# Two halves of three rounds for four pairs of rounds: regrouping the small-tile transforms of a spectral filter beside an MLP

## The chip, the cores and the metric

The kernel runs on one core of a Trainium2 chip. The metric is the device time of one execution in microseconds, as the median of several runs. The core has a matrix engine (TensorE, PE in the profile, with its weight loads shown apart as PEld), VectorE (DVE), ScalarE (ACT), GpSimd (POOL) and a queue engine (SyncE, SP) that issues the DMAs here, those that transpose among them. TensorE writes to PSUM, eight banks of 512 float32 per partition; the other engines copy from there.

## The reference

```python
def _A_ref(x, w_r, w_i):
    X = rfft2(x.astype(float32), axes=(-2, -1))
    X = X * (w_r + 1j * w_i)
    return irfft2(X, s=(S, D), axes=(-2, -1)).astype(bfloat16)

def _B_ref(x, w1, b1, w2, b2):
    h = gelu(einsum("bsd,df->bsf", x, w1) + b1)      # tanh form
    return einsum("bsf,fd->bsd", h, w2) + b2

xn = layernorm(x)                                    # x: 1 x 2048 x 640, bfloat16
return x + _A_ref(xn, w_r, w_i) + _B_ref(xn, w1, b1, w2, b2)   # F = 1536
```

The output is the sum of the input, a spectral filter of its normalized form and a two-layer MLP of the same normalized form.

## The kernel before

The 2048 rows lie in 16 tiles of 128 rows. Every operation has a name with its tile, pair of tiles or group, and a table (`ORDER`) says by hand in which order each of the five engines issues its operations; a second table (`SLOTS`) says which PSUM bank or piece of on-chip memory each buffer gets. `Plan.sync` works out the waits: an operation waits for the writers of what it reads and for the last users of the memory that it writes. Nothing is scheduled beyond that: if an operation waits, all behind it on its engine wait too.

Normalization and transposes. `st`, `ag`, `ve`, `rs`, `nm` normalize a tile (VectorE, with a little on GpSimd). Tiles 0 to 5 are transposed by TensorE (`tp`) and copied (`tc`), tiles 6 to 15 by DMA on the SP queue (`td`), into `xnT`.

The MLP. `h` is layer 1, in blocks of tiles (`BLOCKS`): a matmul takes 128 rows of W1 by 128 features as weights and streams 128 columns for each tile of the block; `ge` is the gelu on ScalarE. `k` and `l` are layer 2. For the tiles of `KEEP` it runs early and is stored (`k`, added to the input by `kk` on VectorE); for the others (`l`) it stays in PSUM until the filter's last matmul (`fin`) adds to it. A group of `k` or `l` is three matmuls of 512 columns and three of 128.

The filter. The two-dimensional transform is made of matmuls with tables:

- `f1`, `f2` fold the rows (VectorE), `G` is a transform over the 128 rows of a tile, `gx` copies its result to `XV`.
- `b0` to `b5` transform along the width, for two or three tiles at a time (`GROUPS`); each fills the four low PSUM banks, and two copies `xb` (one for two banks) empty them into `Xb`.
- `c` finishes the transform across tiles, by matmuls of 32 x 32 weights. The array of TensorE holds sixteen such tiles at once, so a pass is 16 matmuls that run side by side. Before, four tiles of the 16 (`P` = 0 to 3) form a round pair: `cP.0` and `cP.1`, each of two passes of 322 columns that add up in the four low banks. Each round is emptied by two copies `y`.
- `m` multiplies with the complex filter, `z` sums the products (VectorE).
- `d` goes back across tiles, in two rounds of two passes of 320 columns for each `P`; `u` empties them, and `vt` turns the tiles by DMA on the SP queue into `XV`.
- `e0` to `e5` transform the width back, for the tiles of `GROUPS`, again into the four low banks; they need all sixteen turned tiles. `yo` empties a group, `y2` and `yf` unfold it (VectorE), `fin` is the last transform, and `os` adds all up on VectorE before the store `out`.

Since `b`, `c`, `d` and `e` all use the four low banks, one of them can begin only when the copies of the one before it in the order have ended. Between them the order puts layer 1 (in the high banks) and layer 2 as work that fills the time. At the start, 42 matmuls on zeros (`idle0`) run until the first tile is normalized; the first number of `WARM` counts them.

## Time and profile before

| | |
|---|---|
| median of 3 runs | 149.25 us (148.64 to 151.17) |
| profiled execution | 149.7 us, of which the span is 148.4 |
| TensorE busy | 144.8 us, 1847 matmuls |
| VectorE busy | 110.9 us, 242 instructions |
| ScalarE busy | 82.9 us, 161 instructions |
| layer 1, 256 columns | 300 matmuls |
| small-tile transforms | 512 matmuls in 16 rounds |

The span is the time from the first to the last instruction that the profiler recorded; the execution's own time is 1.3 us longer. Busy times of TensorE overlap, as matmuls are pipelined: for what a stretch costs one takes the distance from its first start to the next stretch's. In a timeline row the first number is the start, the second the length from the first start to the last end, then the engine, the line, the operation with its result and its operands, the tile of the array, the shape and the count. A bracket at the end says how long the engine was idle before the row, and for whom. Weight loads are rows of PEld and overlap the matmuls. A row of SPq is the queue's work of issuing; a DMA lands later.

### The profile page before, as it was taken

The numbers are of one execution on the slowest core, as the hardware profiler recorded it, in microseconds if no ns is written. First come the engines' busy times: TensorE is split into PE (matmuls) and PEld (weight loads), VectorE is DVE, ScalarE is ACT, GpSimd is POOL, SyncE is SP. The second block draws the span as 40 slices with busy tenths as digits, with TensorE's granted clock in tenths as the row PEclk, the third lists the DMA queues.
The fourth block names the chain that finished last, engine by engine and source line by source line (L and its number), as shares of the span: only waits on it lengthen the run. The fifth ranks groups of instructions, "written<-read, shape, count | busy, mean of one in ns | idle before, by whom it ended". The sixth has DMA issues, their size and how long they took to land.

```text
span 148.4 us, 4311 instructions
## 1 busy us (share of the span) xinstructions
PE 144.8 (98%) x1847; PEld 99.4 (67%) x1847; DVE 110.9 (75%) x242; ACT 82.9 (56%) x161; POOL 7.0 (5%) x18
## 2 busy tenths in 40 slices
PE   7999999999999999999999999999999999999994
PEld 7989888888868766666554534345676665655564
DVE  2888999999997799498659759700098898968743
ACT  3649889998984775994555467891624204000000
POOL 2003030222200000000000000000000000000000
DMA  4899999366997993004200460645001122101333
GB/s 133 293 326 406 306 269 178 60 93 164 299 203 128 213 210 134 4 4 88 44 4 7 88 133 4 133 92 115 19 4 44 44 88 95 44 0 49 133 111 110
DMA packets 27882, 18.07 MB, mean 122 GB/s; under 512 B 18904, under 2 KB 26584, under 8 KB 27736
## 3 DMA queue, kind: packets, MB, share of 16 engines
q1 hardware_dynamic: 27840, 17.81, 48.8%
q8 instruction: 14, 0.23, 0.6%
q14 instruction: 4, 0.03, 0.1%
q10 hardware_dynamic: 24, 0.00, 0.0%
HBM read 10.92 MB, written 2.62 MB: 91 GB/s over the span
## 4 chain that ended last, share of the span: by engine, by line
PE 70%; DVE 13%; DMA 6%; SPq 5%; issue 2%; ACT 2%; POOL 1%
PE ps L403 70%; DMA X<-in_A_x_dram 6%; SPq L398 5%; DVE stats L508 4%; DVE T L564 3%; DVE T L560 2%; ACT Xb L413 2%; DVE Z L537 1%; DVE mv L510 1%; POOL rstd L519 1%; DVE T L537 1%; DVE ve L518 0%; DVE U L537 0%; DVE W L772 0%
## 5 line engine op out<-in xcount | busy, mean ns | idle before, releaser
L403 PE MATMUL ps<-xnT,W 128*128 128x256 bf16 (+2 forms) x480 | 58.7, 274 | 0.3 <-DMA W<-in_B_w_dram 0.3
L403 PE MATMUL ps<-W,gT 128*128 128x128 bf16 (+4 forms) x408 | 57.9, 291 | 0.0
L403 PEld LDWEIGHTS ps<-xnT,W 128*128 128x128 bf16 x480 | 40.2, 98 | 12.4 <-issue 1.9
L619 ACT ACTIVATE gT<-ps,b1col 128x256 bf16<-128x256 f32 (+2 forms) x96 | 39.3, 483 | 10.8 <-PE ps L403 10.6
L403 PEld LDWEIGHTS ps<-W,gT 128*128 128x128 bf16 x408 | 30.4, 98 | 22.3 <-issue 1.7
L508 DVE BATCH_NORM_STATS2 stats<-X 128x6 f32<-128x320 bf16 x32 | 14.4, 476 | 2.6 <-DMA X<-in_A_x_dram 2.6
L733 DVE TENSOR_TENSOR Wf<-Wf 128x960 bf16<-128x960 bf16 (+1 forms) x12 | 6.8, 597 | 11.8 <-ACT Wf L413 11.7
L413 ACT ACTIVATE Wf<-ps 128x960 bf16<-128x960 f32 (+1 forms) x8 | 6.9, 902 | 12.8 <-PE ps L403 12.8
L413 ACT ACTIVATE Xb<-ps 128x960 bf16<-128x960 f32 (+1 forms) x9 | 9.8, 1138 | 7.0 <-PE ps L403 7.0
L676 DVE TENSOR_TENSOR T<-Y,Wf 128x1288 bf16<-128x1288 bf16 x16 | 12.4, 824 | 0.5 <-ACT Y L413 0.4
L413 ACT ACTIVATE Y<-ps 128x644 bf16<-128x644 f32 x12 | 8.1, 715 | 3.9 <-PE ps L403 3.9
L761 DVE TENSOR_TENSOR xnT<-ps,X 128x640 f32<-128x640 f32 x8 | 6.6, 820 | 4.7 <-PE ps L403 4.7
L772 DVE TENSOR_TENSOR W<-ps,X 128x640 bf16<-128x640 f32 (+2 forms) x10 | 6.9, 687 | 3.8 <-PE ps L403 3.8
L564 DVE TENSOR_TENSOR T<-T 128x512 bf16<-128x512 bf16 (+1 forms) x32 | 9.1, 312 | 0.2
L413 ACT ACTIVATE XV<-ps 128x1280 bf16<-128x1280 f32 x7 | 8.7, 1243 | 0.1
L772 DVE TENSOR_TENSOR W<-ps,xnT 128x640 bf16<-128x640 f32 x8 | 6.5, 820 | 1.8 <-PE ps L403 1.7
L403 PE MATMUL ps<-getab,XV 32*128 32x160 bf16 (+1 forms) x128 | 7.5, 242 | 0.0
L519 POOL TENSOR_TENSOR rstd<-ve,mhalf 128x2 f32<-128x2 f32 (+1 forms) x8 | 6.1, 763 | 31.1 <-DVE ve L518 31.1
L738 DVE TENSOR_TENSOR Wf<-Wf 128x960 bf16<-128x960 bf16 (+1 forms) x12 | 6.7, 596 | 0.8 <-PE ps L403 0.7
L403 PEld LDWEIGHTS ps<-getab,XV 32*128 32x128 bf16 (+1 forms) x128 | 6.4, 146 | 1.2
L403 PE MATMUL ps<-etab,XV 32*128 32x160 bf16 (+1 forms) x128 | 7.2, 232 | 0.0
L680 DVE TENSOR_TENSOR Z<-T 128x644 bf16<-128x644 bf16 x16 | 7.0, 488 | 0.1
(52 smaller groups left out, 111.6 us busy)
## 6 DMA issues: line engine op xcount, KB each, us to landing
out_dram<-W SPq DMA_DIRECT2D x15, 160.0 KB, 1.8
X<-in_A_x_dram SPq DMA_DIRECT2D x7, 320.0 KB, 8.2
W<-in_B_w_dram SPq DMA_DIRECT2D x10, 192.0 KB, 5.6
W<-in_B_w_dram SPq DMA_DIRECT2D x2, 960.0 KB, 8.7
Wf<-in_A_w_i_dram SPq DMA_DIRECT2D x7, 160.5 KB, 3.9
Wf<-in_A_w_r_dram SPq DMA_DIRECT2D x7, 160.5 KB, 4.5
gtab<-c_G SPq DMA_DIRECT2D x1, 512.0 KB, 7.8
htab<-c_H SPq DMA_DIRECT2D x1, 512.0 KB, 5.0
```

The lines of the kernel that those rows point to most:

```text
L398: return K.op(name, q, lambda e, _: e.dma_start(dst, src), reads=reads, writes=[buf], after=after, dma=sem or name, gate=gate)
L403: ins = e.matmul(o_, lhsT=lw, rhs=rh, start=st, stop=sp_, skip_group_check=True)
L413: return e.activation(dst(), src(), ACT.Copy)
L508: K.op(f"st{c}.{h}", "dve", lambda e, _, c=c, h=h: e.bn_stats(stats[:, c, 6 * h:6 * h + 6], view(X, c * D + H2 * h, [[1, H2]])), reads=[B_ ...
L519: K.op(f"rs{c0}", "pool", lambda e, _, a=a, b=b: e.tensor_tensor(out=rstd[:, a:b], in0=ve[:, a:b], in1=mhalf[:, a:b], op=ALU.pow), reads=[ ...
L564: ring_ops.append(K.op(f"f2{pair}.{k}{i}", "dve", lambda e, _, op=op, x1v=x1v, xfv=xfv, o_=o_, o0=o0, o1=o1, w=w: e.tensor_tensor(out=xfv( ...
L619: K.op(f"ge{bi}.{fc}", "act", lambda e, _, c0=c0, nt=nt, fc=fc, f0=f0, hps=hps: e.activation(gT[:, fc, 128 * c0:128 * (c0 + nt)], psb(hps. ...
L676: filt_ops.append(K.op(f"m{pair}.{k}", "dve", lambda e, _, k=k, Y=Y, TB=TB, pair=pair: e.tensor_tensor(out=view(TT, TB.slot * 8 * KP + k * ...
L680: K.op(f"z{pair}.{r}", "dve", lambda e, _, TB=TB, Z=Z, r=r, op=op: e.tensor_tensor(out=view(Zb, Z.slot * 4 * KP + r * KP, [[2 * KP, 2], [1 ...
L733: K.op(f"y2{gi}.{k}", "dve", lambda e, _, k=k, op=op, yo=yo, y2=y2, n=n: e.tensor_tensor(out=view(Wf, Y2 + y2.slot * 3 * D + (H2 - 1) * k, ...
L738: K.op(f"yf{gi}.{k}", "dve", lambda e, _, k=k, op=op, y2=y2, yf=yf, n=n: e.tensor_tensor(out=view(Wf, YF + yf.slot * 3 * D + (D - 1) * k, ...
L772: K.op(f"os{c}.{o0}", "dve", lambda e, _, c=c, os_=os_, fps=fps, o0=o0, w=w, kept=kept, base=base, home=home if kept else None: e.tensor_t ...
```

## The change

The small-tile transforms are regrouped. Instead of four `P` with two rounds each, there are two halves of two `P` each, and a half has three rounds in `c` and three in `d`. A bank of 512 columns, of which a round had filled 322, now gets up to 484: the first round of a half holds the first part of `P0` and the first 162 columns of its second part, the next holds the remaining 160 and the first part of `P1`, the third holds the second part of `P1` alone. So c0.0, c0.1, c1.0, c1.1 and likewise for `d` have 64 matmuls in four passes, c0.2, c1.2, d0.2, d1.2 have 32 in two. In `d` the pieces are 320 + 160, 160 + 320 and 320 columns.

The products lose a temporary: `m1` goes to the buffer T, `m0` is made in place in Y, and `z` sums in place in Y. A pool of six buffers takes the place of those for Y and Z; there are four places for `xb` instead of two, four for `u` instead of three and four for normalized pairs instead of five. The zero matrix of `idle0`, the identity and the row of biases share a tile with the table of `b` (EB), and the statistics and b2 share one with a `u` buffer (U3). GpSimd zeroes the padding of `xb` in eight small pieces instead of two.

Tiles 8 to 11 are one block of layer 1, so 60 matmuls of 512 columns stand for 120 of 256. The groups of `b` and `e` are (0,3), (3,3), (6,2), (8,3), (11,3), (14,2), so that the first has three tiles and the third two. `idle0` has 38 matmuls. Some copies move between ScalarE and VectorE: both copies of b1 are VectorE's, both of b4 ScalarE's, those of b2 are shared. The order of all engines is new.

```diff
-BLOCKS = [(0, 1), (1, 1), (2, 2), (4, 2), (6, 2), (8, 2), (10, 2), (12, 4)]
+BLOCKS = [(0, 1), (1, 1), (2, 2), (4, 2), (6, 2), (8, 4), (12, 4)]
-GROUPS = [(0, 2), (2, 3), (5, 3), (8, 3), (11, 3), (14, 2)]
+GROUPS = [(0, 3), (3, 3), (6, 2), (8, 3), (11, 3), (14, 2)]
-BYPE = ()
-WARM = (42, 4)
+WARM = (38, 4)
...
+pe:l0.0.0 pe:e0 pe:l0.0.3 dve:yo0.0 act:yo0.1 dve:y20.0 pe:e1 dve:y20.1 pe:l0.0.6 dve:yf0.0 act:yo1.1 dve:yf0.1 pe:l0.0.9 act:yo1.0 pe:fin0.0 pe:e2
+dve:os0.0 dve:y21.1 sp:out0.0 pe:l6.0.0 act:yo2.1 dve:y21.0 act:yo2.0 pe:l6.0.3 dve:yf1.0 dve:yf1.1 pe:l6.0.6 dve:y22.1 pe:fin3.0 dve:y22.0 dve:os3.0
...
+        EB = sb("EB", [128, 4 * KP])
+        etab, warm, ident, b1t = EB, EB[:, 800:928], EB[:, 928:1056], EB[0:NFC, 1056:1184]
...
-        TT = sb("T", [128, 11 * D])
-        Zb = sb("Z", [128, 2 * 4 * KP])
-        U2 = sb("U2", [128, 2 * D])
+        TT = sb("T", [128, 32 * KP + 2 * D])
+        U2 = sb("U2", [128, 4 * KP])
         PS = es.enter_context(nc.psum_tensor("ps", [128, 8 * 512], F32))
 
+        XB = [(xb3, 0, 3), (xb3, 6 * KP, 3), (U2, 0, 2), (EB, 0, 2)]
...
-            ("xn", 5), ("x1", 1), ("xf", 2), ("xb", 2), ("y", 2), ("t", 2), ("z", 2), ("u", 3))]
+        p_xn, p_x1, p_xf, p_xb, p_yz, p_t, p_u = [Pool(k, n) for k, n in (
+            ("xn", 4), ("x1", 1), ("xf", 2), ("xb", 4), ("yz", 6), ("t", 2), ("u", 4))]
...
+        def yz(Y):
+            return 8 * KP + 2 * D + 4 * KP * (Y.slot + 4 if Y.slot < 2 else Y.slot - 2)
...
+        def products(pair):
+            Y, TB = Ys[pair], TBs[pair]
+            m1 = K.op(f"m{pair}.1", "dve", lambda e, _: e.tensor_tensor(
+                out=view(TT, TB.slot * 4 * KP, [[2 * KP, 2], [KP, 2], [1, KP]]), in0=yv(Y, True), in1=wv(pair, 1), op=ALU.mult),
+                reads=[Y, B_w, B_wpad], writes=[TB], after=ring_ops)
+            m0 = K.op(f"m{pair}.0", "dve", lambda e, _: e.tensor_tensor(out=yv(Y, False), in0=yv(Y, False), in1=wv(pair, 0), op=ALU.mult),
+                reads=[Y, B_w, B_wpad], writes=[Y], after=[m1])
+            filt_ops.extend([m1, m0])
+            for r, op in enumerate((ALU.subtract, ALU.add)):
+                def sums(e, _, r=r, op=op):
+                    rows = view(TT, yz(Y) + r * KP, [[2 * KP, 2], [1, KP]])
+                    return e.tensor_tensor(out=rows, in0=rows, in1=view(TT, TB.slot * 4 * KP + r * KP, [[2 * KP, 2], [1, KP]]), op=op)
+                K.op(f"z{pair}.{r}", "dve", sums, reads=[TB, Y], writes=[Y], after=[m0])
...
+        CUT, c_ops = 162, []
+        for half in range(2):
+            P0, P1 = 2 * half, 2 * half + 1
+            for n, pieces in enumerate(([(P0, 0, 0, KP), (P0, 1, 0, CUT)], [(P0, 1, CUT, KP - CUT), (P1, 0, 0, KP)], [(P1, 1, 0, KP)])):
+                cps = K.buf(f"cps{half}_{n}", psum, 4, LOW)
+                at, bank = [0, pieces[0][3]], [[], []]
+                c_ops.append(pe(f"c{half}.{n}", lambda pieces=pieces, cps=cps, at=at: [
+                    (psb(cps.slot + 2 * pp + hi, [[1, w]], at[k], 64 * qq + 32 * (lo ^ pp), 32),
                      part(mtab, 64 * hi + 32 * lo, 32, (P == pp == qq == hi == lo == 0) * 128 + v * 64 + r * 32, [[1, 32]]),
+                     part(xb_at[4 * P + 2 * pp + qq][0], 64 * hi + 32 * lo, 32, xb_at[4 * P + 2 * pp + qq][1] + v * KP + c0, [[1, w]]), v == 0 and k == 0, v == 1)
+                    for v in range(2) for k, (P, r, c0, w) in enumerate(pieces) for pp, qq, hi, lo in tiles],
+                    reads=list({id(B_xb[c]): B_xb[c] for P in sorted({p[0] for p in pieces}) for c in range(4 * P, 4 * P + 4)}.values()) + [B_xbpad, B_m] + ([B_xbpad3] if half else []), writes=[cps]))
+                for P in sorted({p[0] for p in pieces}):
+                    mine = [(at[k], r, c0, w) for k, (q, r, c0, w) in enumerate(pieces) if q == P]
+                    o_, r, c0, w = mine[0][0], mine[0][1], mine[0][2], sum(p[3] for p in mine)
+                    for pp in range(2):
+                        Y = Ys[2 * P + pp]
+                        bank[pp].append(K.op(f"y{2 * P + pp}.{len(Y.writers)}", "act dve",
+                             copy(lambda Y=Y, r=r, c0=c0, w=w: view(TT, yz(Y) + r * KP + c0, [[2 * KP, 2], [1, w]]),
+                                  lambda cps=cps, pp=pp, o_=o_, w=w: psb(cps.slot + 2 * pp, [[512, 2], [1, w]], o_)), reads=[cps], writes=[Y], after=(ring_ops if P else []) + bank[pp]))
+            for pair in range(4 * half, 4 * half + 4):
+                products(pair)
+            for n, pieces in enumerate(([(P0, 0, 0, 2), (P0, 1, 0, 1)], [(P0, 1, 1, 1), (P1, 0, 0, 2)], [(P1, 1, 0, 2)])):
+                dps = K.buf(f"dps{half}_{n}", psum, 4, LOW)
+                at, bank = [0, Q4 * pieces[0][3]], [[], []]
+                pe(f"d{half}.{n}", lambda pieces=pieces, dps=dps, at=at: [
+                    (psb(dps.slot + 2 * pp + qq, [[1, Q4 * w]], at[k], 64 * hi + 32 * lo, 32),
                      part(ntab, 64 * qq + 32 * (lo ^ pp), 32, (P == pp == qq == hi == lo == 0) * 96 + 32 * ((0, 2), (1, 0))[v][r], [[1, 32]]),
+                     part(TT, 64 * qq + 32 * (lo ^ pp), 32, yz(Ys[2 * P + pp]) + (2 * hi + r) * KP + v + i0, [[1, w], [2, Q4]]), r == 0 and k == 0, r == 1)
+                    for r in range(2) for k, (P, v, i0, w) in enumerate(pieces) for pp, qq, hi, lo in tiles],
+                    reads=[Ys[2 * P + pp] for P in sorted({p[0] for p in pieces}) for pp in range(2)] + [B_n], writes=[dps])
+                for P in sorted({p[0] for p in pieces}):
+                    mine = [(at[k], 2 * v + i0, w) for k, (q, v, i0, w) in enumerate(pieces) if q == P]
+                    o0, g, w0 = mine[0][0], mine[0][1], sum(p[2] for p in mine)
+                    for pp in range(2):
+                        U = Us[2 * P + pp]
+
+                        def evac(e, name, U=U, dps=dps, pp=pp, o0=o0, g=g, w0=w0):
+                            for o_, w in ((0, 128), (512, 32)):
+                                ins = copy(lambda: uv(U, o_ + w * g, [[D, 2], [w, w0], [1, w]]), lambda: psb(dps.slot + 2 * pp, [[512, 2], [Q4, w0], [1, w]], o0 + o_ // 4))(e, name)
+                            return ins
+                        bank[pp].append(K.op(f"u{2 * P + pp}.{len(U.writers)}", "act dve", evac, reads=[dps], writes=[U, B_us[2 * P + pp]],
+                                             after=a_ops + ring_ops + xs_ops + c_ops[:3] + bank[pp]))
+            for pair in range(4 * half, 4 * half + 4):
+                turn(pair)
```

On TensorE, at the end of the rounds of `d`, before (Z and ntab are the operands of `d`; xnT and W belong to layer 1, W and gT to layer 2):

```order
213 L403 MATMUL ps<-Xb,mtab 32x322 x32
214 L403 MATMUL ps<-xnT,W 128x512 x5
215 L403 MATMUL ps<-Z,ntab 32x320 x32
216 L403 MATMUL ps<-xnT,W 128x512 x5
217 L403 MATMUL ps<-Z,ntab 32x320 x32
218 L403 MATMUL ps<-xnT,W 128x512 x20
219 L403 MATMUL ps<-Z,ntab 32x320 x32
220 L403 MATMUL ps<-xnT,W 128x512 x5
221 L403 MATMUL ps<-Z,ntab 32x320 x32
222 L403 MATMUL ps<-xnT,W 128x512 x20
```

and after, where T holds the products:

```order
237 L397 MATMUL ps<-T,ntab 32x320 x16
238 L397 MATMUL ps<-T,ntab 32x160 x16
239 L397 MATMUL ps<-T,ntab 32x320 x16
240 L397 MATMUL ps<-T,ntab 32x160 x16
241 L397 MATMUL ps<-xnT,W 128x512 x15
242 L397 MATMUL ps<-T,ntab 32x160 x16
243 L397 MATMUL ps<-T,ntab 32x320 x16
244 L397 MATMUL ps<-T,ntab 32x160 x16
245 L397 MATMUL ps<-T,ntab 32x320 x16
246 L397 MATMUL ps<-xnT,W 128x512 x16
247 L397 MATMUL ps<-T,ntab 32x320 x32
248 L397 MATMUL ps<-xnT,W 128x512 x19
```

A round with 320 columns in two passes has become one with passes of 320 and 160 in turn, and the layer-1 work between the rounds has changed: after the last of 64 (rows 242 to 245, d1.1) come 16 matmuls, the last small round (d1.2) and 19 more, where before d3.1 was followed by 20 and then by layer 2.

On TensorE at the first two groups of the way back (getab and XV belong to `e`), before, from e0 on; three more pairs of layer 2 follow until e1 in row 261:

```order
248 L403 MATMUL ps<-getab,XV 128x160 x16
249 L403 MATMUL ps<-W,gT 128x512
250 L403 MATMUL ps<-W,gT 128x128
251 L403 MATMUL ps<-W,gT 128x512
252 L403 MATMUL ps<-W,gT 128x128
253 L403 MATMUL ps<-W,gT 128x512
254 L403 MATMUL ps<-W,gT 128x128
```

and after, from e0 to e1:

```order
279 L397 MATMUL ps<-getab,XV 128x160 x24
280 L397 MATMUL ps<-W,gT 128x512
281 L397 MATMUL ps<-W,gT 128x128
282 L397 MATMUL ps<-W,gT 128x512
283 L397 MATMUL ps<-W,gT 128x128
284 L397 MATMUL ps<-W,gT 128x512
285 L397 MATMUL ps<-W,gT 128x128
286 L397 MATMUL ps<-getab,XV 128x160 x24
```

e0 has three tiles (24 matmuls) where it had two (16), and three pairs of layer 2 stand between e0 and e1 where there were six.

On the SP queue, before, from tile 10's transpose to the last of them (W is W2 here, Wf the filter, etab the table of `b`):

```order
18 L541 DMA_TRANSPOSE xnT<-T 128x5x128
19 L398 DMA W<-in_B_w_dram 128x6x640
20 L398 DMA Wf<-in_A_w_i_dram 16x5136
21 L398 DMA Wf<-in_A_w_r_dram 16x5136
22 L398 DMA etab<-c_E 128x800
23 L398 DMA Wf<-in_A_w_r_dram 16x5136
24 L541 DMA_TRANSPOSE xnT<-T 128x5x128
25 L541 DMA_TRANSPOSE xnT<-Z 128x5x128 x2
26 L541 DMA_TRANSPOSE xnT<-U 128x5x128 x2
```

and after, from tile 6 on, with the first six loads behind:

```order
16 L540 DMA_TRANSPOSE xnT<-T 128x5x128 x6
17 L392 DMA Wf<-in_A_w_r_dram 16x5136
18 L392 DMA Wf<-in_A_w_i_dram 16x5136
19 L392 DMA EB<-c_E 128x800
20 L392 DMA Wf<-in_A_w_i_dram 16x15x321
21 L392 DMA W<-in_B_w_dram 128x6x640
22 L392 DMA Wf<-in_A_w_i_dram 16x16x321 x2
```

The transposes of tiles 10 and 11 now follow that of tile 9 directly, and those of tiles 12 to 15 stand seven rows further on (row 29), behind all loads of the filter.

267 lines of the change are left out of this document (110 added, 157 removed).

## The prediction

> **What bounds the kernel now.** I read the first and second parts of the profile's page (busy time by engine, the span in slices), then the chain of waits that ended last, then the TensorE timeline, stretch by stretch.
>
> ```profile
> PE 144.8 (98%) x1847; PEld 99.4 (67%) x1847; DVE 110.9 (75%) x242; ACT 82.9 (56%) x161; POOL 7.0 (5%) x18
> PE   7999999999999999999999999999999999999994
> PE 70%; DVE 13%; DMA 6%; SPq 5%; issue 2%; ACT 2%; POOL 1%
> ```
>
> ```profile
> 59.64 25.33 PE ps L403 x433
> 84.99 61.47 PE ps L403 x648
> ```
>
> TensorE is busy in every slice from the second on, and the chain's two longest pieces are TensorE alone, from 59.64 us to 146.46 of a span of 148.4. So a change of this kernel is worth what it takes out of TensorE's stream, plus the waits that it opens or closes there; vector and scalar work counts only where a matmul waits for it.
>
> **Paces.** What a row of the stream costs is the distance to the start of the next row; durations overlap.
>
> ```profile
> 22.10 5.08 PE L403 MATMUL ps<-xnT,W 128*128 128x256 bf16 x45
> 27.08 0.45 PE L403 MATMUL ps<-gtab,T 128*128 128x128 bf16 x5
> ...
> 60.90 1.26 PE L403 MATMUL ps<-xnT,W 128*128 128x256 bf16 x10
> 62.08 0.49 PE L403 MATMUL ps<-Xb,mtab 32*32 32x322 bf16 x32
> 62.51 1.27 PE L403 MATMUL ps<-xnT,W 128*128 128x256 bf16 x10
> 63.70 0.51 PE L403 MATMUL ps<-Z,ntab 32*32 32x320 bf16 x32
> 64.15 1.26 PE L403 MATMUL ps<-xnT,W 128*128 128x256 bf16 x10
> ...
> 87.41 1.25 PE L403 MATMUL ps<-xnT,W 128*128 128x512 bf16 x5
> 88.59 0.51 PE L403 MATMUL ps<-Z,ntab 32*32 32x320 bf16 x32
> ...
> 90.67 4.49 PE L403 MATMUL ps<-xnT,W 128*128 128x512 bf16 x20
> 95.08 0.51 PE L403 MATMUL ps<-Z,ntab 32*32 32x320 bf16 x32
> ```
>
> Layer 1, 256 columns: 45 take 4.98 us and 10 take 1.18, so 35 take 3.80, 0.1086 each; the ten lose 1.18 - 1.086 = 0.094 going into a round. 512 columns: 20 take 4.41, 5 take 1.18, so 0.2153 each, and again some 0.10 at the entry. A round of 32 small matmuls costs 0.43 (62.08 to 62.51) or 0.45 (63.70 to 64.15), 0.44 in the mean, and 0.095 before it: 0.535.
>
> **1. Rounds.** Sixteen rounds go: 16 x 0.535 = 8.56 us. Twelve come: four like the old (2.14), eight of 64 matmuls in four passes over the 16 tiles, two of 320 or 322 columns and two of 160 or 162. The two new passes cost at least their columns: by the pace of 256, (162 / 256) x 0.109 = 0.069 each, so 0.58 a round. They cost at most what a whole old round takes, 0.44 more, so 0.88 a round. Between these the loads of new tile weights decide:
>
> ```profile
> L224 PEldq EVENT_SEMAPHORE  x1: 1095/1095/1095, 62.5 to 62.5; - x1
> ...
> 63.70 0.19 PEld L403 LDWEIGHTS ps<-Z,ntab 32*32 32x32 bf16 x32 [0.21 <-issue]
> ```
>
> The load queue was held at a semaphore until about 63.6, yet 32 weights were in within 0.19 us: 16 need some 0.095, a little over a short pass. I take 0.60, near the column bound, which the loads hardly exceed. Eight rounds: 8 x (0.60 + 0.095) = 5.56, all twelve 7.70: **-0.85** (-1.0 by the columns, +1.4 by the old round's length). The evacuations of up to 968 elements instead of 644 lie on ScalarE and VectorE beside layer matmuls that need neither.
>
> The Trainium skill ("TensorE: Matmul & The Clock Gate", section "Wait — 56ns, not 53.3ns?") states a floor of about 25 ns from one matmul's start to the next, however few columns. By it a round of 64 takes at least 1.6 us and the change loses. The trace disagrees: 32 in 0.43 us are 13 ns apart, in different tiles of the array.
>
> **2. Layer 1 of tiles 8 to 11.** 120 matmuls at 0.1086 (13.03) become 60 at 0.2153 (12.92): **-0.1**. Twelve fewer gelu calls on ScalarE, which is idle 44% of the span, bring nothing by themselves.
>
> **3. Waits that go.** Two stand in the rows.
>
> ```profile
> 8.97 3.25 PE L403 MATMUL ps<-xnT,W 128*128 128x128 bf16 x55 [0.27 <-DMA W<-in_B_w_dram]
> 59.64 0.50 PE L403 MATMUL ps<-Xb,mtab 32*32 32x322 bf16 x32 [0.26 <-ACT Xb L413]
> 57.20 2.38 ACT L413 ACTIVATE Xb<-ps 128x960 bf16<-128x960 f32 x2 [1.62 <-PE ps L403]
> ```
>
> The new order reaches the fifth piece of W1 three quarters of a microsecond later, and the two copies of group 2 are split over ScalarE and VectorE now: **-0.5** for both. What shows next at the start is the four idle matmuls less: the first transpose still waits for the first normalized tile, so they give nothing.
>
> ```profile
> 3.74 1.91 PE L403 MATMUL ps<-warm 128*128 128x128 bf16 x16
> 5.52 0.71 PE L549 MATMUL ps<-ident,Z 128*128 128x128 bf16 x5
> 6.03 0.63 PE L403 MATMUL ps<-warm 128*128 128x128 bf16 x4
> ...
> 5.02 0.45 DVE L537 TENSOR_SCALAR Z<-X,mv,rstd 128x640 bf16<-128x640 bf16 x1
> ```
>
> TensorE stands still 0.4 us before 5.52 instead. It is slow there already (five transposes from 5.52 to 6.03, 0.10 each, where 55 from 8.97 on take at most 3.25, 0.06 each), so at worst the fast pace starts some 20 matmuls later: 0 to +0.9, taken as 0. The other small waits of the old order (none over 0.25) I let the new order's own small ones replace.
>
> **4. Waits that come.** (a) Groups 1 and 4 (b1, b4) have both copies on one engine, VectorE for the one and ScalarE for the other. c0.0 must have both copies of b1; d0.0 needs the banks of b4. Behind b1 stand 2.46 us of matmuls at the paces above plus an entry of 0.09, behind b4 2.11 plus 0.09. By the ScalarE row above two copies take 2.38, and with some 0.17 around them 2.55; VectorE's cost about as much each:
>
> ```profile
> L413 ACT ACTIVATE Xb<-ps 128x960 bf16<-128x960 f32 x6 | 7.3, 1259 | 5.3 <-PE ps L403 5.3
> L414 DVE CAST Xb<-ps 128x960 bf16<-128x960 f32 x2 | 2.5, 1246 | 0.8 <-PE ps L403 0.8
> ```
>
> That is 2.55 - 2.20 = 0.35 at d0.0 and (2 x 1.25 + 0.17) - 2.55 = 0.12 at c0.0, 0.2 with an addition of b2 that may still run on VectorE: **+0.55** (0 to 1.0). Queued behind a waiting c0.0 is all of TensorE.
>
> (b) Block (8,4) begins with h5.1.0, which needs tiles 8 to 11 at once; tile 11's transpose, before the sixth issue after tile 10's, follows it directly.
>
> ```profile
> 32.66 1.28 SPq L541 DMA_TRANSPOSE xnT<-T  x1
> ...
> 37.04 1.29 SPq L541 DMA_TRANSPOSE xnT<-T  x1
> ...
> xnT<-T SPq DMA_TRANSPOSE x4, 3.3
> xnT<-Z SPq DMA_TRANSPOSE x4, 4.9
> ```
>
> Counted along the new VectorE order, tile 10 is normalized some 1.6 us earlier than now, so its transpose goes at about 31, tile 11's at 32.3, and lands 3.3 later at 35.6 at most; TensorE, counted along its new order, arrives at 35.0 to 35.4. **+0.2** (0 to 1.4, were the queue no earlier than now or the landing that of the second row).
>
> (c) The inverse width transform e0 needs all 16 turned tiles.
>
> ```profile
> 90.84 0.77 ACT L413 ACTIVATE gtab<-ps 128x512 bf16<-128x512 f32 x2 [0.86 <-PE ps L403]
> ...
> 99.51 2.60 SPq L700 DMA_TRANSPOSE XV<-gtab  x2
> 102.15 1.28 SPq L700 DMA_TRANSPOSE XV<-U  x1
> ...
> XV<-U SPq DMA_TRANSPOSE x6, 2.6
> 105.21 1.02 PE L403 MATMUL ps<-getab,XV 128*128 128x160 bf16 x16
> ```
>
> Now the last transpose lands at 102.15 + 2.6 = 104.75 and e0 does not wait (105.21). Afterwards the last eight all stand behind d1.1, which completes the first of them: from its start about 0.75 to the end of the round, 0.45 for the copy, then seven more issues at 1.32 (2.64 / 2) and 2.6 of landing, 13.0 to 13.2. TensorE has 12.7 to 12.85 there (rounds d1.1 and d1.2, 35 layer-1 matmuls, five groups of layer 2): **+0.35** (0 to 0.7).
>
> (d) e0 now makes three tiles, and e1 needs its banks emptied, with one group of layer 2 (six matmuls) between them. Before, e0 was smaller and two groups followed; e1, of three tiles, shows what such a group needs.
>
> ```profile
> 107.81 1.38 PE L403 MATMUL ps<-getab,XV 128*128 128x160 bf16 x24
> 109.12 0.99 PE L403 MATMUL ps<-W,gT 128*128 128x512 bf16 x6
> 109.94 0.43 PE L403 MATMUL ps<-Wf,htab 128*128 128x512 bf16 x2
> 109.36 1.15 DVE L414 CAST Wf<-ps 128x960 bf16<-128x960 f32 x1
> ```
>
> By these, banks filled from 107.81 on are empty at 109.36 + 1.15 = 110.51, 2.70 later, while 1.31 of e and 0.82 of layer 2 make 2.13 of work: **+0.5** (0.3 to 0.8). Nothing after it makes up for that, since TensorE is what ends last.
>
> **Sum** against the profiled 149.7 us (span 148.4, 1.3 around it): -0.85 - 0.1 - 0.5 + 0.55 + 0.2 + 0.35 + 0.5 = +0.15, so about 149.85. That execution is 0.45 above the median of 149.25, so 149.4 on the scale of the medians.
>
> **Rivals.**
> *The new waits are hidden.* Two copies on one engine, the landing and the last transposes are each within 0.5 us of being early. If (a), (b) and (c) vanish, 1.1 goes: 148.3; if (d) halves and the rounds reach the column bound, 147.9; with the small old waits gone unreplaced, 147.3. For it: TensorE arrives late everywhere if one earlier wait already held it. Against: (d) has a hard row. 0.22.
> *Rounds are fed no faster than now.* Place: each of the eight. If 64 matmuls take twice 0.44, eight take 7.8 and the twelve 9.94: slower by 1.4 than the sixteen, 151.7 in all. It decides from 0.71 us a round, where 8 x (0.71 + 0.095) + 2.14 is 8.58. For it: two weights per tile and bank group have to be exchanged in passes half as long. Against: the 0.19 us of the load row. 0.12, and of that 0.02 for the skill's floor, which by its 1.6 us a round would give about 157.
> *Block (8,4) and e0 come late together.* Tile 11's landing at 4.9 instead of 3.3 and the copies of d1.1 behind gelu calls: +1.2 and +0.35 on the sum, 151.0. For it: the loads that crowd the same queue. Against: in the new order these loads stand behind tile 11. 0.11.
> *The change is not what it says* (as many rounds, or waits from the sharing of tiles that serialize it): the instruction counts exclude the first; the second is in (a). No chance of its own.
>
> **Numbers.** Forecast 0.55, 148.6 to 150.4. The range takes the hidden-wait case down to 147.4 and the two late cases up to 151.4. About 2% is what a measurement can tell from no change: 146.3 and 152.2. Below the one lies only a sum of all gains and no new wait, 0.04; above the other the doubled rounds together with one late wait, or the clock, 0.06; between 0.90.
>
> **What would show it.** Right: rounds of 64 cost 0.58 to 0.65 from start to next row, eight of them; a TensorE wait of some 0.5 before e1 on VectorE's or ScalarE's copy, and one before e0 on the last transpose; no 0.27 at the fifth piece of W1. Wrong: rounds of 0.8 or more; waits before h5 over 1 us; a slow pace of 128-column matmuls after 8 us; or no wait at e0 and e1 and a span under 147.

## The result, and the profile after

| | before | after |
|---|---|---|
| median | 149.05 us (6 runs, 148.64 to 151.17) | 154.50 us (6 runs, 153.14 to 154.91) |
| ratio | 1 | 1.0349 (95%: 1.0293 to 1.0405) |
| profiled execution, span | 149.7, 148.4 us | 153.14, 151.8 us |

The change costs 3.5%. The profiled execution of after is the shortest of its six, so its trace shows less than the median lost; the first experiment shows a longer one. All ratios leave out executions more than 1.5% above the kernel's fastest, among them the profiled ones of the first two experiments.

The page of after: the busy times and TensorE in 40 slices.

```profile
PE 144.6 (95%) x1911; PEld 94.6 (62%) x1911; DVE 109.6 (72%) x238; ACT 80.7 (53%) x153; POOL 7.4 (5%) x24
PE   7799999999999999999999997999889999999994
```

TensorE is busy for 144.6 us, as before (144.8), but its share has gone from 98% to 95%: it stands still for some 3.6 us more, and three slices in the second half (7, 8, 8) show where. The chain of waits, which before was TensorE alone from 59.64 us on, shows what it stands still for (start, length, what):

```profile
87.33 4.48 DMA XV<-T
...
92.91 0.58 ACT gT L618
...
105.84 2.65 DMA XV<-U
...
110.02 1.17 DVE Wf L408
...
111.32 38.47 PE ps L397 x359
```

TensorE ends at 111.32 + 38.47 = 149.79 instead of 84.99 + 61.47 = 146.46, 3.3 later. The places, in its timeline (a row's cost is the distance to the next start):

```profile
10.31 2.52 PE L397 MATMUL ps<-xnT,W 128*128 128x128 bf16 x42 [0.30 <-DMA W<-in_B_w_dram]
...
35.44 5.77 PE L397 MATMUL ps<-xnT,W 128*128 128x512 bf16 x27 [0.26 <-ACT gT L618]
...
53.19 0.83 PE L397 MATMUL ps<-Xb,mtab 32*32 32x322 bf16 x64
53.95 1.27 PE L397 MATMUL ps<-xnT,W 128*128 128x256 bf16 x10
...
67.93 0.85 PE L397 MATMUL ps<-T,ntab 32*32 32x320 bf16 x64 [0.26 <-ACT Xb L407]
68.71 1.80 PE L397 MATMUL ps<-W,gT 128*128 128x512 bf16 x12
...
79.54 0.56 PE L397 MATMUL ps<-T,ntab 32*32 32x160 bf16 x40
80.41 0.41 PE L397 MATMUL ps<-T,ntab 32*32 32x160 bf16 x24 [0.31 <-issue]
...
93.54 1.25 PE L397 MATMUL ps<-xnT,W 128*128 128x512 bf16 x5 [0.86 <-ACT gT L618]
...
108.54 1.42 PE L397 MATMUL ps<-getab,XV 128*128 128x160 bf16 x24 [0.68 <-DMA XV<-U]
...
111.32 1.39 PE L397 MATMUL ps<-getab,XV 128*128 128x160 bf16 x24 [0.45 <-DVE Wf L408]
```

A round of 64 costs 0.76 (c0.0, 53.19 to 53.95) to 0.78 (d0.0, 67.93 to 68.71), not 0.60. With the prediction's 0.095 at each entry that is 8 x (0.77 + 0.095) = 6.92, and 9.06 with the four small rounds: against 8.56 before **+0.5**, where the prediction had -0.85. The rest by place, beside the prediction's terms:

| place | predicted | this execution |
|---|---|---|
| the rounds | -0.85 | +0.5 |
| layer 1 of tiles 8 to 11, merged | -0.1 | taken over as -0.1, not measured alone |
| fifth piece of W1; copies at c1.0 | -0.5 | +0.03 (0.30 for 0.27); -0.26 |
| c0.0; d0.0 | +0.2; +0.35 | 0 (no wait at 53.19); +0.33 |
| h5.1.0, tile 11 | +0.2 | +0.26 |
| a stop inside d0.1 (1.21 for 0.77); one inside c1.2 (0.65 for 0.43) | none | +0.44; +0.22 |
| h6.3.0, before d1.1 | none | +1.0 (0.86 idle, and an entry) |
| e0 | +0.35 | +0.68 |
| e1 | +0.5 | +0.45 |
| the start | 0 | -0.5 |
| sum | +0.15 | +3.05, of 3.3 seen |

The start is ahead: by 12.67 TensorE has done ten transposes and 99 matmuls of layer 1, before the change ten and 96 by 13.00. Its first five transposes take 0.29 us (5.53 to 5.82) and took 0.51 (5.52 to 6.03).

Two of the places need a second look at other engines. The hold at h6.3.0 is a full bank: the gelu that should empty it stands on ScalarE behind the copy u5.0, which waits 3.31 us for a DMA (ScalarE's timeline of after):

```profile
91.88 1.03 ACT L407 ACTIVATE T<-ps 128x768 bf16<-128x768 f32 x2 [3.31 <-DMA XV<-T]
```

Pair 5 writes the `u` buffer that pair 1 had, so it waits until tiles 2 and 3 are turned out of it. All eight transposes of the first half begin with one issue at 82.23, since they wait for d0.1, and those two go as the third and fourth of them:

```profile
82.23 1.20 SPq L684 DMA_TRANSPOSE XV<-U  x1
83.47 2.49 SPq L684 DMA_TRANSPOSE XV<-gtab  x1
86.01 2.60 SPq L684 DMA_TRANSPOSE XV<-T  x2
```

Before, three of the eight had gone long ahead of the others:

```profile
66.89 2.55 SPq L700 DMA_TRANSPOSE XV<-U  x2
69.49 1.28 SPq L700 DMA_TRANSPOSE XV<-gtab  x1
```

And the rounds: the 64 weight loads of d0.0, in two stretches of the load queue (stretch, length and busy time, loads active, clock, DMA), and the one load between them.

```profile
67.92:68.06 0.14, 0.14 (x32) 1.00 0.00 0
...
68.27:68.53 0.26, 0.26 (x31) 1.00 0.00 0
```

```profile
68.08 0.09 PEld L397 LDWEIGHTS ps<-T,ntab 32*32 32x32 bf16 x1
```

Two sets of 16 go in at once, in 0.14 us, as the 32 of an old round did. The first load of the third set follows at 68.08, when the second pass begins. The other 31 go in only from 68.27 on, 8.3 ns apart, 0.13 us for sixteen. The starts of the four passes are 67.93, 68.08, 68.27 and 68.41 in the single records: the third begins 0.18 after a pass of 160 columns that by the prediction's pace needs 0.07, and the load that begins the rest of its set starts 4 ns after it.

### The profile page after: what moved, and what is told of

The parts are those of the page before. It is cut to its first block, busy times and chain, and to the rows that moved or that the text cites. A ratio compares the mean times of both kernels' runs of the same rounds, so it can differ in the third digit from the quotient of the medians.

```text
span 151.8 us, 4432 instructions
## 1 busy us (share of the span) xinstructions
PE 144.6 (95%) x1911; PEld 94.6 (62%) x1911; DVE 109.6 (72%) x238; ACT 80.7 (53%) x153; POOL 7.4 (5%) x24
## 4 chain that ended last, share of the span: by engine, by line
PE 75%; DMA 8%; ACT 6%; DVE 5%; SPq 3%; issue 1%; POOL 0%; ACTq 0%
PE ps L397 74%; DMA X<-in_A_x_dram 4%; DMA XV<-T 3%; ACT gT L618 3%; SPq L392 2%; DMA XV<-U 2%; ACT Xb L407 2%; DVE U L507 1%; DVE T L669 1%; DVE T L672 1%; ACT XV L407 1%; DVE Wf L408 1%; SPq L684 1%; PE ps L548 1%; ACT T L407 1%
## 5 line engine op out<-in xcount | busy, mean ns | idle before, releaser
L397 PEld LDWEIGHTS ps<-xnT,W 128*128 128x128 bf16 x420 | 34.1, 98 | 17.5 <-ACT gT L618 2.3
L507 DVE BATCH_NORM_STATS2 U<-X 128x6 f32<-128x320 bf16 x32 | 13.9, 471 | 3.7 <-DMA X<-in_A_x_dram 3.7
L407 ACT ACTIVATE T<-ps 128x644 bf16<-128x644 f32 (+6 forms) x18 | 10.7, 649 | 6.7 <-PE ps L397 3.3
L407 ACT ACTIVATE XV<-ps 128x1280 bf16<-128x1280 f32 (+2 forms) x9 | 10.2, 1145 | 0.6 <-PE ps L397 0.6
L563 DVE TENSOR_TENSOR T<-T 128x128 bf16<-128x128 bf16 (+1 forms) x32 | 8.7, 315 | 0.1
L751 DVE TENSOR_TENSOR Wf<-Wf 128x960 bf16<-128x960 bf16 (+1 forms) x12 | 6.8, 597 | 1.6 <-ACT Wf L407 1.4
L536 DVE TENSOR_SCALAR T<-X,mv,rstd 128x640 bf16<-128x640 bf16 x16 | 6.7, 442 | 1.2 <-POOL rstd L518 1.0
L559 DVE TENSOR_TENSOR T<-T 128x640 bf16<-128x640 bf16 x16 | 7.3, 480 | 0.1
L397 PE MATMUL ps<-EB,XV 32*128 32x160 bf16 (+1 forms) x128 | 7.2, 232 | 0.0
L678 DVE TENSOR_TENSOR T<-T 128x644 bf16<-128x644 bf16 x16 | 6.8, 487 | 0.0
```

Of the source, the lines that this page charges most:

```text
L397: ins = e.matmul(o_, lhsT=lw, rhs=rh, start=st, stop=sp_, skip_group_check=True)
L407: return e.activation(dst(), src(), ACT.Copy)
L507: K.op(f"st{c}.{h}", "dve", lambda e, _, c=c, h=h: e.bn_stats(stats[:, c, 6 * h:6 * h + 6], view(X, c * D + H2 * h, [[1, H2]])), reads=[B_ ...
L536: norm_ops.append(K.op(f"nm{c}", "dve", lambda e, _, c=c, n=n, xnv=xnv: e.tensor_scalar(out=xnv(n, 0, [[1, D]]), in0=view(X, c * D, [[1, D ...
L559: K.op(f"f1{pair}.{k}", "dve", lambda e, _, k=k, op=op, xnv=xnv, x1v=x1v: e.tensor_tensor(out=x1v(H2 * k, [[D, 2], [1, H2]]), in0=xnv(0, 0 ...
L563: ring_ops.append(K.op(f"f2{pair}.{k}{i}", "dve", lambda e, _, op=op, x1v=x1v, xfv=xfv, o_=o_, o0=o0, o1=o1, w=w: e.tensor_tensor(out=xfv( ...
```

## The experiments

Medians, and the ratio to before on the same chip with its 95% interval; kernels of one chip stand together.

| kernel | chip | median us | ratio |
|---|---|---|---|
| after again | 6 | 155.48 | 1.0342 (1.0287 to 1.0397) |
| new order of the first eight turns | 6 | 154.29 | 1.0326 (1.0278 to 1.0373) |
| last short pass 32 columns; half of its tiles | 6 | 155.61; 154.73 | one run each |
| W2's second half earlier as well | 4 | 153.04 | 1.0220 (1.0129 to 1.0311) |
| and e1, h5.1.0 moved ("mended") | 4 | 152.31 | 1.0199 (1.0147 to 1.0251) |
| 12 more idle matmuls; first short pass 32 columns | 4 | 156.06; 156.05 | one run each |
| mended, again | 4 | 151.65 | 1.0153 (1.0065 to 1.0240) |
| mended, two turns less | 4 | 151.17 | 1.0131 (1.0047 to 1.0215) |
| mended, passes as before | 4 | 151.05 | 1.0110 (1.0060 to 1.0159) |
| mended, copies of b4 split | 4 | 153.74 | 1.0291 (1.0218 to 1.0363) |
| mended, again | 3 | 152.49 | 1.0261 (1.0233 to 1.0289) |
| mended, sixteen rounds | 3 | 153.41 | 1.0312 (1.0286 to 1.0337) |
| mended, again | 0 | 153.10 | 1.0237 (1.0193 to 1.0281) |
| mended, sixteen rounds, two waits less | 0 | 152.09 | 1.0180 (1.0135 to 1.0225) |

**After, once more, and the turns in another order.** The first is the changed kernel as it is. The second takes the turns of pair 1 first (of `ORDER`, only the names of the SP queue):

```diff
-sp:vt4 sp:vt0 sp:vt2 sp:vt3 sp:vt6 sp:vt1 sp:vt7 sp:vt5
+sp:vt2 sp:vt3 sp:vt0 sp:vt1 sp:vt4 sp:vt6 sp:vt7 sp:vt5
```

> The changed kernel again, beside the experiments. Profiled before: TensorE ends at 149.8 us, a round of 64 takes 0.76 to 0.78 us, 1.0 us is lost at h6.3.0 (93.5 us), 0.85 before e0, 0.6 before e1. If the losses are fixed by the order, each comes back here within 0.2 us; if the 1.5 us by which other runs were longer than the profiled one is one place, this profile can show it. Time 153 to 155.

> Only the order of the first eight turning DMAs is changed: those of pairs 1 and 0 first (vt2 vt3 vt0 vt1), the other pairs behind. Theory U (the copy u5.0 waits for vt3 because pair 5 reuses the buffer of pair 1, and ScalarE's gelu calls stand behind it): vt3 lands near 87 instead of 91.8, the 3.3 us of idle ScalarE before u5.0 go, h6.3.0 is not held, the last eight DMAs start no earlier than d1.1 allows, time 1.0 to 1.5 us shorter. Rival (the hold at h6.3.0 comes from ScalarE's own load): no change within 0.3 us.

The profiled run of after took 156.37 us, 3.2 more than the first one. Its TensorE timeline has the same waits, most of them longer (so they do not come back within 0.2 us as expected), and a new one, for W2:

```profile
36.20 5.56 PE L397 MATMUL ps<-xnT,W 128*128 128x512 bf16 x26 [1.00 <-DMA xnT<-T]
46.01 1.80 PE L397 MATMUL ps<-W,gT 128*128 128x512 bf16 x12 [0.42 <-DMA W<-in_B_w_dram]
...
82.31 0.41 PE L397 MATMUL ps<-T,ntab 32*32 32x160 bf16 x24 [0.77 <-issue]
...
96.80 1.11 PE L397 MATMUL ps<-T,ntab 32*32 32x160 bf16 x64 [0.93 <-ACT gtab L407]
...
111.67 1.43 PE L397 MATMUL ps<-getab,XV 128*128 128x160 bf16 x24 [1.47 <-DMA XV<-U]
```

In the first row one of the 27 matmuls has no record, so the wait there is some 0.8 and not 1.00. The hold for ScalarE moved to d1.1 itself here (96.80), with the same cause one turn later: u5 waits for pair 1, u4 for pair 0. With the turns in the new order it is gone. ScalarE's timeline of that kernel shows u5.0 waiting for its round and no longer for a DMA:

```profile
94.58 1.03 ACT L407 ACTIVATE T<-ps 128x768 bf16<-128x768 f32 x2 [1.86 <-PE ps L397]
```

and TensorE enters d1.1 without a wait. Five of the six traces of kernels with the old order of turns have such a hold (the one with 12 more idle matmuls has none), and none of the nine with the new order and rounds of 64 or 48. So the reuse of the buffers, with the turns in that order, makes the hold. That it is worth 1.0 us of time is not shown: the ratio went from 1.0342 to 1.0326, within the intervals. This kernel's profiled execution lost more elsewhere: TensorE's row of that place, and three stretches from there on (length and busy time, matmuls, granted clock, DMA share, GB/s).

```profile
47.49 2.18 PE L397 MATMUL ps<-W,gT 128*128 128x512 bf16 x12 [2.83 <-DMA W<-in_B_w_dram]
```

```profile
47.50:49.50 2.00, 2.00 (x13) 0.82 1.41 228
49.50:52.00 2.50, 2.29 (x26) 0.50 1.11 62
52.00:54.00 2.00, 1.88 (x18) 0.96 1.31 92
```

TensorE stood 2.83 us for the second half of W2, and after it the clock fell to half: (1 - 0.82) x 2 / 0.5, all of 2.5 and (1 - 0.96) x 2 / 0.5 make 3.4 us at 0.50. What changed for that load is its place on the SP queue. Its issue and its landing, before:

```profile
L398 SPq DMA_DIRECT2D W<-in_B_w_dram x1: 585/585/585, 34.0 to 34.0; - x1
...
DMA to landing us min/median/max: 6.2/6.2/6.2
```

and in the kernel with the turns in the new order:

```profile
L392 SPq DMA_DIRECT2D W<-in_B_w_dram x1: 596/596/596, 36.0 to 36.0; - x1
...
DMA to landing us min/median/max: 11.4/11.4/11.4
```

It is issued 2 to 3 us later, directly behind the four loads (three of the filter, one of the table of `b`) that stood behind it before, and ten more loads of the filter follow at once; before, the next came 9 us after those four. In the seven traces of kernels that have it in this place it landed 7.5 to 11.4 us after its issue, and layer 2's first group that needs it waited 0 to 2.8 us.

**Why a round of 64 takes 0.77.** Three kernels change one kind of short pass and nothing else; each leaves out part of the result. In the first, the short pieces have only 32 columns in the last of their two passes; in the second, that pass has all columns, but 8 of its 16 tiles; in the third, the first short pass has 32 columns. The edits in `c`, and the same were made in `d`:

```diff
-(psb(cps.slot + 2 * pp + hi, [[1, w]], at[k], 64 * qq + 32 * (lo ^ pp), 32),
+(psb(cps.slot + 2 * pp + hi, [[1, w if w > 170 or not v else 32]], at[k], 64 * qq + 32 * (lo ^ pp), 32),
...
-for v in range(2) for k, (P, r, c0, w) in enumerate(pieces) for pp, qq, hi, lo in tiles]
+for v in range(2) for k, (P, r, c0, w) in enumerate(pieces) for pp, qq, hi, lo in tiles if w > 170 or not v or not lo]
...
+(psb(cps.slot + 2 * pp + hi, [[1, w if w > 170 or v else 32]], at[k], 64 * qq + 32 * (lo ^ pp), 32),
```

> In every round of 64 the last pass of short pieces (the second that adds up) has 32 columns instead of 160 or 162: part of the filter's sum is left out. Theory C (a pass takes its columns): a round falls by 128 columns, 0.055 us, from 0.77 to 0.71. Theory L (a pass takes the loading of its 16 weights, 8.3 ns each in the trace): no change, 0.77.

> In every round of 64 the last pass of short pieces has 8 of its 16 tiles (lo = 0) at full width: part of the filter's sum is left out. Theory C: a pass of the same columns, no change, 0.77. Theory L: eight weights less at 8.3 ns, a round falls by 0.067 to 0.70.

> In every round of 64 the first pass of short pieces has 32 columns instead of 160 or 162 (part of the sum is left out). The last pass narrowed gave 0.055 less a round, as by its columns; half of its tiles gave 0.01. Theory C (columns): again 0.055 less a round. Theory R (the pass behind it cannot start before its weights are reloaded, 0.18 us after the short pass began): no change, 0.77.

c0.0 and what follows it, in the timelines of the first, the second and the third:

```profile
55.02 0.78 PE L397 MATMUL ps<-Xb,mtab 32*32 32x322 bf16 x64
55.73 1.27 PE L397 MATMUL ps<-xnT,W 128*128 128x256 bf16 x10
```

```profile
56.34 0.82 PE L397 MATMUL ps<-Xb,mtab 32*32 32x322 bf16 x56
57.09 1.27 PE L397 MATMUL ps<-xnT,W 128*128 128x256 bf16 x10
```

```profile
55.53 0.83 PE L397 MATMUL ps<-Xb,mtab 32*32 32x322 bf16 x64
56.29 1.27 PE L397 MATMUL ps<-xnT,W 128*128 128x256 bf16 x10
```

0.71, 0.75 and 0.76, against 0.76. In c0.0 the short passes are the second and the fourth. The fourth costs what its columns cost: 130 fewer save 0.05, half of its loads 0.01. The second costs the same with a fifth of its columns.

In c0.1 the short passes are the first and the third, and the answer is another. The record of the matmul behind it is missing in these three traces, so the distance to the one after that is compared: it is 0.99 in after and 0.99 in the first variant, 0.92 in the second (the first row of the round and the one behind it) and 0.97 in the third.

```profile
61.64 0.40 PE L397 MATMUL ps<-Xb,mtab 32*32 32x160 bf16 x24
...
62.56 2.39 PE L397 MATMUL ps<-W,gT 128*128 128x128 bf16 x17 [0.16 <-issue]
```

Here 130 columns fewer in the third pass save nothing, and eight loads fewer save 0.07, which is 8 x 8.3 ns. So a short third pass costs the loading of its weights, and a short fourth pass its columns. Besides, in all eight rounds of after the third pass begins 0.18 to 0.19 us after the second, whether that has 160, 162, 320 or 322 columns, and in c0.0 also with 32. What it waits for in that time is not shown: its first weights are in early, and the rest go in when it has begun. Neither of the two theories in the expectations, columns or loads, holds for every pass. A round of 0.77 is the rival which the prediction called "Rounds are fed no faster than now" in its milder form: past 0.71, short of 0.88.

**The load of W2.** Turns as above, and the load directly behind the transpose of tile 11:

```diff
-act:ge4.10 sp:W00p
+act:ge4.10 sp:w2_1 sp:W00p
...
-pe:h5.0.0 sp:w2_1 dve:st15.1
+pe:h5.0.0 dve:st15.1
```

> The order of the turning DMAs as in the run before, and the second half of W2 issued directly behind tile 11's transpose instead of four loads later. Theory W (the layer-2 group k1.6 waits for W2's second half, which is crowded by the burst of filter loads: it landed 6.2 us after its issue before the change, 7.5 to 11.4 after): it lands near 42, the wait of 0 to 3.0 us at k1.6 is gone in every run, and with it most of the spread; time 1 to 2.5 us shorter than the run before. Rival (the queue is slow there whatever stands in it, so that the loads that follow only change places): some other wait of like size appears between 40 and 60 us.

```profile
DMA to landing us min/median/max: 5.9/5.9/5.9
```

That is again the time from the issue, at 34.2, to the landing: 5.9 us, as before the change, and 5.3 to 6.0 in the ten traces with the load in this place. Fourteen loads follow it at once here, so those behind it are not what delays it. With the four ahead of it it is slow; why is not shown. Layer 2 does not wait, and with both repairs the ratio is 1.022 for 1.034, on another chip and with intervals that overlap a little.

**The first groups of the way back.** In addition, six more matmuls of layer 2 go ahead of e1, and a part of layer 1 for tiles 6 and 7 ahead of h5.1.0. This kernel, "mended" in the table, is the base of what follows.

```diff
-pe:e1 dve:y20.1 pe:l0.0.6
+pe:l0.0.6 pe:e1 dve:y20.1
...
-pe:h5.1.0 sp:W10n
+pe:h4.5.3 pe:h5.1.0 sp:W10n
```

> As the run before, and two groups of layer 2 between e0 and e1 instead of one, and four layer-1 matmuls of tiles 6 and 7 ahead of h5.1.0. By the waits read in the traces: 0.5 at e1 and 0.2 at h5.1.0 go, 0.6 shorter than the run before. Rival: the wait at e1 comes back at fin0.0 or e2, no change.

> The kernel of the run with the four edits of order again, as the measure for the three runs beside it: 151.9 to 152.8; before e0 a wait of about 1.0 us, rounds of 64 at 0.77.

The wait at e1 went and came back at e2, whose copies are both on ScalarE (TensorE's row in the kernel's second profile, which is like the first):

```profile
113.42 1.08 PE L397 MATMUL ps<-getab,XV 128*128 128x160 bf16 x16 [0.59 <-ACT Wf L407]
```

A wait of 0.45 for one of 0.6: moving work between these `e` groups moved the wait. The other edit did not do what was expected either: a wait at h5.1.0 shows in three of the four traces of this kernel (0.41 to 0.86 in the row, of which some 0.2 is a matmul without a record). The same kernel gave 151.65 to 153.10 on three chips, so only kernels of one chip are compared below.

**The last turned tile.** Two of the last eight turns (tiles 12 and 13) are left out, and so is that part of the result.

```diff
                 q = 2 * pair + qq
+                if q in (12, 13):
+                    continue
```

> As e8, without the last two turning DMAs (tiles 12 and 13 of the way back keep what lay there: part of the result is left out). Theory T (e0 waits for the chain of eight DMAs that all stand behind d1.1): the chain is 2 x 1.3 us shorter, the wait before e0 is gone, 1.0 us shorter than e8. Rival (e0 also waits for its banks or for layer 1's gelu calls, or the time comes back at e2): less than 0.4 us shorter.

The group of `e` on TensorE on the page, mended and with two turns less; the last number is idle time and for what most of it:

```profile
L397 PE MATMUL ps<-getab,XV 32*128 32x160 bf16 (+1 forms) x128 | 7.6, 243 | 1.8 <-DMA XV<-U 1.2
```

```profile
L397 PE MATMUL ps<-getab,XV 32*128 32x160 bf16 (+1 forms) x128 | 7.6, 242 | 0.6 <-ACT Wf L407 0.6
```

The wait of 1.2 us at e0 is gone, so the queue of eight transposes behind d1.1 made it. The median fell only 0.5, within the spread of the two; what the removal is worth in time is not settled.

**The regrouping by itself, from two sides.** First, the mended kernel without the last short pass, as many passes as before in twelve rounds (that part of the sum is left out of the result); then the mended kernel with sixteen rounds again, in the new order and with all else new.

```diff
-for v in range(2) for k, (P, r, c0, w) in enumerate(pieces) for pp, qq, hi, lo in tiles]
+for v in range(2) for k, (P, r, c0, w) in enumerate(pieces) for pp, qq, hi, lo in tiles if w > 170 or not v]
...
-([(P0, 0, 0, KP), (P0, 1, 0, CUT)], [(P0, 1, CUT, KP - CUT), (P1, 0, 0, KP)], [(P1, 1, 0, KP)])
+([(P0, 0, 0, KP)], [(P0, 1, 0, KP)], [(P1, 0, 0, KP)], [(P1, 1, 0, KP)])
```

> As e8, without the last pass of short pieces in each round of 64 (part of the filter's sum is left out), so that there are 32 passes over the tiles as before the change, in 12 rounds, and 1.8 us of columns less in none but these. Theory P (a pass costs about 0.16 us whatever its width): a round of three passes takes 0.60 to 0.62 and the kernel is 1.2 us shorter than e8. Theory C (a short pass costs its columns): 0.70, 0.55 us shorter. If the end is set by the chain of DMAs before e0 and not by TensorE's work, the part of the gain behind d1.1 is lost.

> As e8, but the regrouping alone undone: four rounds of 32 in each half and transform, sixteen in all, with everything else of the change kept (blocks, groups, buffers, products in place); the order between c0.1 and e0 had to be written anew. Theory P (passes cost alike, and rounds that mix two P hold the turning DMAs back): rounds 16 x 0.53 = 8.5 us instead of 9.04, the wait before e0 falls from 1.1 to 1.4 us to under 0.7, the stop inside d0.1 is gone: 0.5 to 1.5 us shorter than e8, by what the new order itself loses. Rival (the regrouping pays, and only the order around it was poor): as long as e8 or longer, by the four entries more (0.4) and the copies of four more rounds.

> The kernel of e8 a third time, as the measure for the run beside it: 151.6 to 152.4.

Without the last short pass a round takes 0.62 to 0.70:

```profile
53.56 0.76 PE L397 MATMUL ps<-Xb,mtab 32*32 32x322 bf16 x48
54.26 1.26 PE L397 MATMUL ps<-xnT,W 128*128 128x256 bf16 x10
```

and the time is 0.6 us less than the mended kernel's, again within the spread. The first kernel with sixteen rounds was slower than the mended one, 153.41 for 152.49, but its own order, which had to be written anew between the rounds, had two waits that the mended kernel does not have:

```profile
75.25 0.96 PE L398 MATMUL ps<-EB,XV 128*128 128x160 bf16 x16 [0.48 <-ACT gtab L408]
...
94.97 2.33 PE L398 MATMUL ps<-xnT,W 128*128 128x512 bf16 x10 [1.04 <-ACT gT L619]
```

The first is a copy of `u` that stood behind two gelu calls on ScalarE, the second a gelu behind two copies of `u`. With these calls moved, and measured beside the mended kernel (six executions of each):

```diff
-act:ge5.6 act:ge5.7 dve:m3.0
+act:u0.1 act:ge5.7 act:ge5.6
...
+pe:h6.1.0 pe:h6.1.3 pe:h6.5.0
```

> As e12, with its two own waits of order mended: 1.04 us before h6.5.0 (its bank's gelu stood behind two copies of u) and 0.5 before b5 (a copy of u behind two gelu calls). Both go, and the kernel is 1.3 to 1.5 us shorter than e12, 151.9 to 152.1, at or a little under e15. Theory P: under e15 by 0.3 to 1.0 us. Rival (the regrouping pays): over e15.

> The kernel of e8 again, as the measure for e14 beside it: 151.6 to 152.5.

152.09 with sixteen rounds, 153.10 with twelve: 1.0 us for the old grouping, although the intervals of the two ratios overlap by a little (1.0193 to 1.0225). The rounds take 0.43 to 0.45 in it, there is no stop in d0.1, and the wait at e0 is still 1.14. So the regrouping is no gain, and by the trace a loss of some 0.5 us and the stop. With it undone 1.8% remain, so the larger part of the cost is in what else the change brought: the order, the buffers, the blocks and groups.

**Copies of b4 on two engines.** One copy of b4 goes from ScalarE to VectorE, and VectorE's copy of b3 ahead of the sums z2.1 and z3.1, a second edit that the expectation does not name.

```diff
-pe:b4 act:ge5.8 dve:kk4 dve:m3.1 pe:h5.7.0 act:xb4.0 dve:m2.1 pe:h5.6.0
-act:xb4.1
+pe:b4 act:ge5.8 dve:kk4 dve:m3.1 dve:xb4.1 pe:h5.7.0 act:xb4.0 dve:m2.1 pe:h5.6.0
...
-pe:b3 dve:z3.0 dve:z2.1 dve:z3.1 pe:k5.9 act:xb3.1 dve:xb3.0
+pe:b3 dve:z3.0 dve:xb3.0 dve:z2.1 dve:z3.1 pe:k5.9 act:xb3.1
```

> As e8, with the two copies of b4 on VectorE and ScalarE instead of both on ScalarE. By the trace the wait at d0.0 is 0.33 us beyond a usual entry: it goes, and the kernel is 0.3 us shorter if VectorE's later copies (b3's before d0.2) are not late for it; if they are, the wait turns up at d0.2 and nothing is gained.

```profile
69.88 1.32 PE L397 MATMUL ps<-EB,XV 128*128 128x160 bf16 x24 [0.33 <-DVE T L408]
73.42 0.52 PE L397 MATMUL ps<-T,ntab 32*32 32x320 bf16 x32 [0.43 <-DVE T L678]
```

The wait at d0.0 is gone, as it should be, and two others stand behind it for VectorE, at b3 (for a copy) and at d0.2 (for the sums that now follow the copy of b3): together 0.76 for 0.33. The two edits cannot be told apart. The median is 2.1 us above the mended kernel's, of which this explains 0.4.

**Twelve more idle matmuls at the start** (the first number of `WARM` 50 instead of 38).

> The changed kernel with 50 idle matmuls at the start instead of 38. Two questions. The start: TensorE's 0.9 us of rest before the first transpose is filled; if the rest costs anything, the first transposes and layer 1 run faster; I expect no change. The stop of 0.5 to 1.0 us inside round d0.1, always after 41 of its 64 weight loads, with no semaphore there: theory I (instruction supply, at a fixed count of instructions) moves it by 12 pairs, to after the 29th load; theory D (something in the data or the banks) leaves it at the 41st.

156.06. The first layer began 0.2 later and ran no faster (51 matmuls in 3.02 us both times), so the shorter start of the change costs nothing. The stop inside d0.1 did what neither theory said: it is neither at the 29th load nor at the 41st, but missing in this one trace.

No kernel here beats the one before. The best with the whole result were the mended one (1.0153 on one chip, up to 1.0261 on another) and the one with sixteen rounds (1.0180).

## Why the prediction was wrong

It said 149.4 with 147.4 to 151.4; the median is 154.5.

**The rounds, the step that failed first.** "I take 0.60, near the column bound, which the loads hardly exceed." The row behind it, 32 loads in 0.19 us, shows two sets, one in use and one waiting. A round of four passes needs a third and a fourth, and nothing in the trace of before shows a third. The step priced it by the speed of the first two. The runs show 0.77: the third pass begins 0.18 us after the second whatever the columns of that, and from then on weights go in 8.3 ns apart. Of some 3.1 us between the forecast and the profiled run, this is 1.35. The rival was on paper, with its break-even at 0.71, and the chance of 0.12 was too low for a term that rested on a row which did not show the case.

**A wait that was not priced: the buffers.** "The second is in (a)" said that the sharing of memory does no more than delay copies. The prediction went over the copies `xb`, but not over the four `u` buffers, in which pair 5 now follows pair 1, while the turns that free them had moved from 66.89 to 82.23 and later. The hold is 1.0 us of TensorE in the profiled run, and the new order of the turns takes it away.

**A wait that was not priced: a load that was moved.** Among the loads moved behind tile 11's transpose the prediction counted the filter's, for what they do to that transpose. The second half of W2 stands among them, and TensorE waits for it: nothing in the profiled execution of after, 0.4 us in the second, up to 2.8 in its variants, and twice the clock on top. Whether it also makes up what lies between 153.1 and the median of 154.5 is not shown; the executions that make the median have no trace.

**Right in mechanism, wrong in size.** (c), the last turned tile: +0.35 predicted, 0.68 in the profiled run, 0.5 to 1.5 in others with that many turns. The chain was taken at 1.32 a turn; in all but one of these traces one of the eight issues took 0.5 to 1.4 longer (that of tile 13, at 105.84 in after, follows the one before it by 1.86). The one without it, with half the tiles in the last short pass, waited 0.49. At the fifth piece of W1 the 0.27 did not go in this execution (0.30), though it did in the other one. In (a) the 0.2 at c0.0 did not come. The start, taken as 0 with up to 0.9 against it, gave 0.5; by the other traces of the changed kernels its pace varies from execution to execution (five transposes take 0.29 in most and 0.51 in two), and how much of the 0.5 the change makes is not shown.

**Right.** d0.0 (+0.33 for 0.35), e1 (+0.45 for 0.5), tile 11 within its bounds of 0 to 1.4 (0.26, some 0.8 in the second run; the row of after names a gelu call, but tile 11 landed at 35.35, forecast 35.6 at most, 0.09 before TensorE went on), and the wait at c1.0 that goes.

**Open.** What the third pass waits for in its 0.18 us, what makes the stops in d0.1 and c1.2, which wait for no semaphore, why W2 lands late behind four other loads, and what part of an execution without a trace is whose.

## What to carry to other kernels

A row of a trace prices only what happened in it: where a change asks a resource for a third of something of which the trace shows two, the bound from the far side is the safer guess (here 0.77, between 0.58 and 0.88). When buffers are shared or transfers move, list for every buffer who has to let go of it and for every moved transfer who waits for it, and price each with the new start times; here the first list would have held 1.0 us beside the 1.35 of the rounds, the second 0 to 2.8 us. And a wait that is mended can come back at the next operation, as that of e1 did at e2.
